# Batch 3's keys turned by transposing transfers instead of TensorE, with K and V blocks four steps apart and scores seven steps behind

## The chip, the core and the metric

The kernel runs on one core of a Trainium2 chip. A core has five engines that each work through a stream of instructions of their own, in order: TensorE (PE; its weight loads are shown as PEld), VectorE (DVE), ScalarE (ACT), GpSimd (POOL) and SyncE (SP). They meet through semaphores. Transfers run on 16 DMA engines; SyncE, ScalarE and GpSimd issue them, each in its place in that engine's stream. The metric is the time of one execution in microseconds (us), so less is better.

## The reference, cut to what matters

Selective attention over 8 batches of 8 heads, 576 positions, head size 64, and then a gated feed-forward network (FFN) on 4608 tokens of 512 values, with 1536 hidden values:

```python
scores = (1 / np.sqrt(D)) * np.matmul(q, k.transpose(0, 1, 3, 2))
cum = np.cumsum(np.maximum(s, 0.0), axis=-1)
bias = -(cum[:, :, :, None] - cum[:, :, None, :])
scores = np.where(causal, -1e9, scores + np.minimum(bias, 0.0))
attn = softmax(scores)                       # over the keys
x = np.matmul(attn, v)                       # to (4608, 512)
xn = x / np.sqrt(np.mean(x * x, axis=-1, keepdims=True) + 1e-6) * rms_g
g = xn @ w_gate
out = (g * sigmoid(g) * (xn @ w_val)) @ w_out
```

Inputs and the output are float32. The kernel multiplies in bf16.

## The kernel before, in words

**The two halves.** The FFN runs over nine chunks of 512 tokens (`ffn`). A chunk has twelve pairs of a gate group (L751) and a value group (L760) of four matmuls each, and then four output groups of twelve matmuls (L773). Between groups the code calls `step()`, 36 times a chunk, 324 times in all. The attention is cut into small pieces, and each step places a few of them. So TensorE's stream is FFN matmuls with pieces of attention between them, and the attention of a batch runs a chunk or two ahead of the FFN that reads it. A step's number is used below as a place in this order: chunk c begins after step 36 c. It is an order written by the program while it is built, not a time; the engines meet it as fast as their waits let them.

**The pieces of a batch.** A batch has five blocks of 128 positions (the last has 64). For each block of keys `kb` and half of the heads `g` there is a score piece (`s_step`, matmuls at L278, exponentials on ScalarE at L302, the causal mask on GpSimd at L311). For each block of queries `qb` and half `g` there is a value product (`av_step`, L344 and L350), whose sum is divided on VectorE (L357, L359). When both halves of a block are there, it is squared and scaled (L366, L379, L382, L389) and turned into the layout of the FFN by a transposing transfer on SyncE's queue (`xt_dma`, L400). The scores read `kqT`, in which K and Q are turned so that the head size lies along the partitions. There is one buffer for scores (`psS`), so a score waits until the exponentials of the one before have read it.

**How K and Q get into `kqT`.** There are three ways, by two constants, `XB = 2` and `KB = 4`:

- Batches 0 and 1: K and Q are loaded in float32 (`kq32`), cast to bf16 (`kqn`), turned on TensorE by four matmuls with an identity (`t_step`, L195; the tail of 64 positions in `tail_step`, L220), and copied out of PSUM by ScalarE or VectorE (L203, L227).
- Batches 2 and 3: Q is loaded in float32, cast on GpSimd (L156) and turned by transposing transfers on SyncE's queue (`kq_dma`, L182). K is loaded in float32, cast on GpSimd (L145), and turned on TensorE, four groups and a tail for a batch, each copied out by ScalarE.
- Batches 4 to 7: Q as in batches 2 and 3. K is loaded block by block by a casting transfer of GpSimd's queue (`load_k`, L162), straight into bf16, and each block is turned by a transposing transfer (`kq_dma` again).

V comes block by block from GpSimd's queue in all batches (`load_v`, L186). `kqn`, `kqT` and `v_sb` have two buffers each, by the parity of the batch.

**What sets the order.** `step()` looks at conditions on step numbers, kept in `done`. `ready(lag, key)` says that something was placed at least `lag` steps ago. Side work stands in four queues (`act_side`, `pool_side`, `dve_side`, `v_side`), of which only the head is looked at, once a step. `casts(b)` fills `pool_side` with the loads of K (`key(c)`) and the casts of Q of batch `b`; `after_av(b)` fills `v_side` with the loads of V of batch `b + 2`. `x_seq` lists the transposing transfers of K and Q, at most one in two steps, and none in a step that places an `xt_dma`. `can_s` and `can_av` hold a score or a product back until its inputs are some steps old:

```python
return all(ready(5, "X", b, 1, c) for c in (kb, min(kb + 1, 4))) and (
    ready(5, "X", b, 0, kb) if b >= KB else ready(3, "T", b) if kb >= 3 else
    all(ready(3, "T", b, hp, 0) for hp in (2 * g, 2 * g + 1)))
```

These lags only decide where an instruction stands. On the chip it still waits for the semaphore of its input, and since the streams are in order, everything behind it waits too. `need(c)` places filler matmuls where the rows for chunk `c` have not been placed in time.

Of the kernel before, what the change touches and what calls it, by code (L numbers as in the profile page):

```python
# [26 lines left out]
def kernel(  # L27
# [13 lines left out]
    B, H, S, D = q.shape  # L41
# [5 lines left out]
    NSC = 5  # L47
# [6 lines left out]
    def rows(c):  # L54
        return 128 if c < 4 else 64
# [25 lines left out]
    kqTn = kqT.rearrange("d a w (h n) -> d a w h n", h=HP)  # L81
    kqTx = kqT.rearrange("d a w (c h n) -> d a w c h n", c=NSC, h=HP)
    XB = 2
    KB = 4
    v_sb = mp.tile([128, 2, NSC, H, NV], BF16, name="v_sb")

    NE = 8
# [72 lines left out]
    def load_k(b, c):  # L160
        n = rows(c)
        nc.gpsimd.dma_start(  # L162
            out=kqn[0:n, b % 2, 0, c],
            in_=k[b, :, c * 128:c * 128 + n, :].rearrange("h p d -> p h d"))
# [19 lines left out]
    def load_v(b, c):  # L184
        n = rows(c)
        nc.gpsimd.dma_start(  # L186
            out=v_sb[0:n, b % 2, c, :, 0:64],
            in_=v[b, :, c * 128:c * 128 + n, :].rearrange("h p d -> p h d"))
# [53 lines left out]
    def slot_free():  # L242
        return eread.get(ecount[0] % NE, 0) == 0
# [5 lines left out]
    def s_step(b, kb, g, pair=None, masked=False):  # L249
# [181 lines left out]

    SLOTS = 36
    K2 = 34
    slot = [0]
    first, chunk = [0], [0]
    done = {}
    last = {"S": -9, "AV": -9, "T": -9, "X": -9, "AVT": -9, "L": -9}
    s_seq = [(b, kb, g) for b in range(B) for kb in range(NSC) for g in (0, 1) if kb < 4 or g == 0]
    s_seq.sort(key=lambda x: (1, 0, x[2], x[1]) if x[0] == 1 and x[1] < 2 else (x[0], x[1], x[2], 0))
    av_seq = [(b, qb, g) for b in range(B) for qb in range(NSC) for g in (0, 1)]  # L440
    xt_seq = [(b, qb) for b in range(B) for qb in range(NSC)]
    t_seq = [(b, hp, w) for b in range(KB) for hp in list(range(HP)) + ["tail"]
             for w in (0, 1) if w == 0 or (hp != "tail" and b < XB)]
# [22 lines left out]
    def early(queue, lag, fns):  # L466

        t = slot[0] + lag
        queue.extend((lambda: slot[0] >= t and phase() < 24, f) for f in fns)

    def check(b, ws=(1, 0)):
        t = slot[0] + (8 if b >= KB else 0)

        def when(w):
            if b < 2:
                return slot[0] % 2 and chunk[0] == b and slot[0] > 16
            return phase() >= 25 and slot[0] >= t and (w == 0 or ready(0, "cast", b, 1))
        dve_side.extend((lambda w=w: when(w), f) for w in (ws if b < KB else (0, 1)) for f in (
            lambda w=w: check_mag(b, w), lambda: check_max(0), lambda: check_max(1),
            lambda w=w: done.__setitem__(("check", b, w), slot[0])))  # L480

    def phase():

        return slot[0] - first[0]

    def loads(b, w, when, lag):

        def main():
            load_kq(nc.scalar, b, w)
            last["L"] = slot[0]  # L490

        def tail():
            load_kq_tail(nc.scalar, b, w)
            done["raw", b, w] = last["L"] = slot[0]
        n = len(act_side)
        when(act_side, lag, [main, tail])
        act_side[n:] = [(lambda c=c: c() and slot[0] - last["L"] >= 3, f) for c, f in act_side[n:]]

    def casts(b):

        def key(c):
            load_k(b, c)
            done["K", b, c] = slot[0]
            if c == NSC - 1:
                check(b)

        def over(w):
            done["cast", b, w] = slot[0]  # L510
            if b + 1 < B and (w == 1 or b + 1 < KB):
                loads(b + 1, w, early, 4)
            if w == 1:
                x_seq.extend((b, ww, c) for c in range(NSC) for ww in ((1, 0) if b >= KB else (1,)))
            else:
                done["cast", b] = slot[0]
                check(b)

        def free(w):
            return ready(0, "check", b - 2, w) and (  # L520
                ready(0, "T", b - 2) if w == 0 and b < KB + 2 else
                b < XB + 2 or ready(4, "X", b - 2, w, 4))
        if b >= KB:
            pool_side.extend((lambda: free(0) and slot[0] % 2 == 0, lambda c=c: key(c)) for c in range(NSC))
        fns = [(1, lambda r=r: cast_x(nc.gpsimd, b, 1, r)) for r in range(NSC)]
        if b == 2:
            fns[-1] = (1, lambda: (cast_x(nc.gpsimd, b, 1, NSC - 1), over(1)))
        else:
            fns += [(1, lambda: over(1))]
        if b < KB:  # L530
            fns += [(0, lambda r=r: cast(nc.gpsimd, b, 0, r, r + 1)) for r in range(NSC)]
            fns += [(0, lambda: over(0))]
        if b == 2:

            def put2(queue, *fs):
                queue.extend((lambda: slot[0] >= K2 and free(0) and free(1), f) for f in fs)
            put2(act_side, *[lambda r=r: cast_x(nc.scalar, b, 1, r) for r in (3, 4)],
                 *[lambda r=r: cast(nc.scalar, b, 0, r, r + 1) for r in (0, 1, 2)])
            put2(pool_side, *[lambda r=r: cast_x(nc.gpsimd, b, 1, r) for r in (0, 1)],
                 lambda: (cast_x(nc.gpsimd, b, 1, 2), over(1)),  # L540
                 lambda: cast(nc.gpsimd, b, 0, 3, 4), lambda: (cast(nc.gpsimd, b, 0, 4, 5), over(0)))
            return
        pool_side.extend((lambda w=w: ready(7, "raw", b, w) and free(w), f) for w, f in fns)

    def after_tail(b):
        if b + 2 < B:
            casts(b + 2)

    def after_av(b):
        if b + 2 < B:  # L550
            if b == 0:
                v_side.extend((lambda: chunk[0] == 1, f) for f in (
                    lambda: (load_v(2, 0), load_v(2, 1)), lambda: (load_v(2, 2), load_v(2, 3)),
                    lambda: (load_v(2, 4), done.__setitem__(("V", 2), slot[0]))))
                return
            early(v_side, 6, [lambda r=r: load_v(b + 2, r) for r in range(NSC)]
                  + [lambda: done.__setitem__(("V", b + 2), slot[0])])

    def do_t(key, **kw):
        b, hp, w = key  # L560
# [58 lines left out]
    def can_s():  # L619
        if not s_seq or not slot_free():  # L620
            return False
        b, kb, g = s_seq[0]
        if b == 1 and (phase() < 24 and phase() % 2 == 0 or kb == 4 and at("AV", 1, 3, 1) > slot[0]):
            return False
        due = SLOTS * ((b * S + kb * 128) // DM) - (26 if b == 1 else 18 if b < 4 else 14)
        if slot[0] - last["S"] < (4 if slot[0] < due - 24 else 3 if slot[0] < due else 2):
            return False
        if b >= XB:
            return all(ready(5, "X", b, 1, c) for c in (kb, min(kb + 1, 4))) and (
                ready(5, "X", b, 0, kb) if b >= KB else ready(3, "T", b) if kb >= 3 else  # L630
                all(ready(3, "T", b, hp, 0) for hp in (2 * g, 2 * g + 1)))
        if kb >= 3 and not ready(3, "T", b):
            return False
        if kb == 4:
            return True
        return all(ready(3, "T", b, 2 * g + j, w) for j in (0, 1) for w in (0, 1))

    def can_av(clear=False):
        if not av_seq:
            return False  # L640
        b, qb, g = av_seq[0]
        if slot[0] - last["AV"] < (1 if (b, qb) == (1, 3) else 2):
            return False
        if b > 0 and g == 1 and slot[0] - last["T"] < 3 and not clear:
            return False
        if b > 1 and not ready(8, "V", b):
            return False
        if qb > 0 and not ready(5, "S", b, qb - 1, g):
            return False
        prev = b * NSC + qb - NX  # L650
        if prev >= 0 and at("XT", prev // NSC, prev % NSC) > slot[0]:
            return False
        return ready(4 if (b, qb) == (1, 3) else 5, "S", b, qb, g)
# [582 lines left out]
```

## Time and profile before

| what | value |
|---|---|
| median of 3 runs | 365.96 us (365.79 to 369.27) |
| the profiled execution | 364.69 us, of which the span of the trace is 363.0 us |
| granted TensorE clock in it | 0.999 |
| TensorE | 2383 matmuls |
| transposing transfers of K and Q (L182) | 50 |
| transposing transfers of normalised rows (L400) | 36 issues in the page's list |
| casting loads of K blocks (L162) | 20 |
| loads of V blocks (L186) | 40 |

In a row of a group of instructions stand the line, the engine, the operation, what is written and read, the shapes, how often, the busy time and the mean of one, and the idle time of the engine just ahead with what ended it. In a row of the timeline stand the start and the length in us. Matmuls overlap, so the start of the next one says more than the length of this one. A row of a transfer gives the queue, how many, the size, and the median time from issue to landing.

### The profile page before, as it was taken

What the parts mean: (1) busy time and instruction counts of PE and PEld (TensorE: products, weight loads), DVE (VectorE), ACT (ScalarE), POOL (GpSimd) and SP (SyncE); (2) the same over time, 40 slices, a digit from 0 to 9 for tenths busy, and PEclk for the clock granted to TensorE, in tenths of its full rate; (3) what the DMA queues carried; (4) which work ended last, traced back from release to release, by engine and by line L of the source; (5) the groups of instructions that cost most, each with busy time, mean ns of one, the idle gap of its engine ahead of it and who ended that gap; (6) DMA issues with size and microseconds to landing.
All of it is one profiled execution on the core that took longest, in us unless ns stands there. A gap on an engine that the chain in (4) does not pass through costs nothing. (4 is left out here: it accounts for less than half of the span.)

```text
span 363.0 us, 6976 instructions
## 1 busy us (share of the span) xinstructions
PE 348.8 (96%) x2383; PEld 160.5 (44%) x2383; DVE 273.4 (75%) x523; ACT 239.8 (66%) x619; POOL 178.2 (49%) x283
## 2 busy tenths in 40 slices
PE   4989999999999999999999999999999999999993
PEld 2445444444445444444444444444444444444441
DVE  6697988698888889788998988884588548827820
ACT  3988884768886778877778768776777653223311
POOL 7959765858865566869737954622232200000000
PEclk9999999999999999999999999999999999999999
DMA  7999999999969399969979994973201130020011
GB/s 228 132 229 256 177 170 259 182 201 193 212 127 138 59 198 138 167 147 163 164 202 124 140 142 105 115 85 90 78 14 17 51 103 1 0 88 29 1 60 60
DMA packets 124096, 45.81 MB, mean 126 GB/s; under 512 B 103956, under 2 KB 118808, under 8 KB 124056
## 3 DMA queue, kind: packets, MB, share of 16 engines
q0 software_dynamic: 62688, 14.29, 47.4%
q1 hardware_dynamic: 51872, 23.80, 32.1%
q10 hardware_dynamic: 9496, 7.23, 8.4%
q8 instruction: 19, 0.31, 0.4%
q14 instruction: 21, 0.17, 0.2%
HBM read 37.90 MB, written 9.44 MB: 130 GB/s over the span
## 5 line engine op out<-in xcount | busy, mean ns | idle before, releaser
L302 ACT ACTIVATE E<-psS,biasK 128x256 bf16<-128x256 f32 (+3 forms) x328 | 107.0, 415 | 18.9 <-PE psS L278 18.6
L751 PE MATMUL psF<-xnT,wg_sb 128*128 128x512 bf16 x432 | 111.1, 379 | 0.6 <-ACT xnT L416 0.3
L760 PE MATMUL psF<-xnT,wv_sb 128*128 128x512 bf16 x432 | 111.1, 379 | 0.0
L773 PE MATMUL psF<-wout_sb,Ht 128*128 128x512 bf16 x432 | 102.5, 379 | 0.1
L763 DVE SCALAR_TENSOR_TENSOR U<-T,psF 128x512 bf16<-128x512 f32 x108 | 73.7, 682 | 29.4 <-ACT T L754 29.4
L754 ACT ACTIVATE T<-psF 128x512 f32<-128x512 f32 x108 | 64.4, 596 | 41.0 <-PE psF L751 38.6
L311 POOL TENSOR_SCALAR_AFFINE_SELECT E<-E 128x512 bf16<-128x512 bf16 x64 | 46.5, 727 | 77.5 <-ACT E L302 77.0
L756 DVE TENSOR_TENSOR Ht<-U,psF 128x512 bf16<-128x512 bf16 x99 | 67.7, 684 | 7.0 <-PE psF L760 0.5
L751 PEld LDWEIGHTS <-wg_sb 128*128 128x128 bf16 x432 | 38.7, 98 | 44.9 <-issue 5.6
L773 PEld LDWEIGHTS <-Ht 128*128 128x128 bf16 x432 | 38.6, 97 | 42.4 <-issue 2.3
L760 PEld LDWEIGHTS <-wv_sb 128*128 128x128 bf16 x432 | 38.5, 98 | 42.2 <-issue 4.2
L778 ACT ACTIVATE osb<-psF 128x512 f32<-128x512 f32 x36 | 21.5, 596 | 32.0 <-PE psF L773 25.5
L389 DVE SCALAR_TENSOR_TENSOR xs_sb<-x_sb,al_all,g_row 128x512 bf16<-128x512 bf16 (+1 forms) x36 | 29.9, 831 | 12.8 <-POOL al_all L382 12.1
L186 POOL DMA_DIRECT2D v_sb<-in_v_dram x40 | 35.4, 888 | 0.7 <-PE psAV L350 0.3
L366 ACT ACTIVATE xs_sb<-x_sb 128x512 bf16<-128x512 bf16 (+1 forms) x37 | 23.5, 636 | 17.9 <-DVE x_sb L359 17.5
L427 DVE TENSOR_TENSOR acc<-acc,mag 128x1280 bf16<-128x1280 bf16 x32 | 26.6, 845 | 0.2
L278 PE MATMUL psS<-kqT 64*128 64x256 bf16 (+2 forms) x304 | 25.9, 256 | 0.9 <-ACT kqT L203 0.5
L350 PEld LDWEIGHTS <-E 128*128 128x128 bf16 x320 | 21.7, 98 | 10.0 <-issue 0.2
L379 POOL TENSOR_SCALAR al_all<-ss_all 128x1 f32<-128x1 f32 (+2 forms) x39 | 10.7, 274 | 29.7 <-ACT xs_sb L366 22.9
L382 POOL TENSOR_TENSOR al_all<-al_all,mhalf 128x1 f32<-128x1 f32 (+2 forms) x39 | 22.2, 570 | 3.2
L344 PEld LDWEIGHTS <-E 128*128 128x128 bf16 x256 | 20.0, 98 | 8.6 <-DVE x_sb L359 1.6
L278 PEld LDWEIGHTS <-kqT 64*128 64x128 bf16 x320 | 9.2, 94 | 30.8 <-issue 29.9
(126 smaller groups left out, 301.0 us busy)
## 6 DMA issues: line engine op xcount, KB each, us to landing
out_dram<-osb SPq DMA_DIRECT2D x36, 256.0 KB, 2.3
kq<-in_q_dram ACTq DMA_DIRECT2D x5, 1024.0 KB, 6.2
v_sb<-in_v_dram POOLq DMA_DIRECT2D x32, 128.0 KB, 6.4
kq<-in_k_dram SPq DMA_DIRECT2D x4, 512.0 KB, 5.6
kq<-in_q_dram SPq DMA_DIRECT2D x4, 512.0 KB, 7.5
kqn<-in_k_dram POOLq DMA_DIRECT2D x16, 128.0 KB, 5.4
wout_sb<-in_moe_w_out_dram POOLq DMA_DIRECT2D x2, 768.0 KB, 9.9
kq<-in_q_dram POOLq DMA_DIRECT2D x1, 1024.0 KB, 10.8
```

The lines of the kernel that those rows point to most:

```text
L186: nc.gpsimd.dma_start(out=v_sb[0:n, b % 2, c, :, 0:64], in_=v[b, :, c * 128:c * 128 + n, :].rearrange("h p d -> p h d"))
L278: nc.tensor.matmul(pair[par][:, j * W:j * W + M], lhsT=kT, rhs=qT, start=(j == 0 and not premask), stop=(j == nj - 1))
L302: nc.scalar.activation(out=eo, in_=ei, func=AF.Exp, scale=0.125, bias=biasK[:, kb, bh:bh + 1])
L311: nc.gpsimd.affine_select(out=Ev[:, :, 0:nq], in_=Ev[:, :, 0:nq], pattern=[[0, nh], [1, nq]], compare_op=ALU.is_ge, fill=0.0, base=0, chan ...
L389: nc.vector.scalar_tensor_tensor(out=xs_sb[0:n, (b * NSC + qb) % NX, :], in0=x_sb[0:n, (b * NSC + qb) % NX, :], scalar=al_all[0:n, col:col ...
L427: nc.vector.tensor_tensor(out=acc[:, sl], in0=acc[:, sl], in1=mag[:, sl], op=ALU.max)
L751: nc.tensor.matmul(Gp, lhsT=wg_sb[:, cc, fs], rhs=xnT[:, cc, x0:x0 + DM], start=(cc == 0), stop=(cc == CC - 1))
L754: nc.scalar.activation(out=T, in_=Gp, func=AF.Tanh, scale=0.5)
L756: nc.vector.tensor_tensor(out=Ht[:, fb - 1, :], in0=pend[0], in1=pend[1], op=ALU.mult)
L760: nc.tensor.matmul(Vp, lhsT=wv_sb[:, cc, fs], rhs=xnT[:, cc, x0:x0 + DM], start=(cc == 0), stop=(cc == CC - 1))
L763: nc.vector.scalar_tensor_tensor(out=U, in0=T, scalar=1.0, in1=Gp, op0=ALU.add, op1=ALU.mult)
L773: nc.tensor.matmul(Op, lhsT=Ht[:, fb, tb * 128:(tb + 1) * 128], rhs=wout_sb[:, fb, :], start=(fb == 0), stop=(fb == FB - 1))
```

## The change

`KB` goes from 4 to 3. Batch 3's K is then handled like that of batches 4 to 7: five casting loads and five transposing transfers in place of one float load with its tail, five casts, five groups of transposes on TensorE and five copies. Batch 3's K loads stand behind its Q casts in `pool_side`; those of batches 4 to 7 stand ahead of the casts, as they did.

A new constant `SPREAD = 4` sets the least number of steps between two blocks of K, and between two blocks of V for batches 4 to 7; for batch 3 blocks of V stay two steps apart. Before, both could go every second step. A product now waits for the V block that it reads and not for the last one of the batch. Scores of batches from `KB` on stand at least seven steps behind the transfers of K and Q that they read, instead of five.

```diff
-    KB = 4
+    KB = 3
...
     K2 = 34
+    SPREAD = 4
...
-    last = {"S": -9, "AV": -9, "T": -9, "X": -9, "AVT": -9, "L": -9}
+    last = {"S": -9, "AV": -9, "T": -9, "X": -9, "AVT": -9, "L": -9, "K": -9, "V": -9}
...
         def key(c):
             load_k(b, c)
+            last["K"] = slot[0]
             done["K", b, c] = slot[0]
...
-        if b >= KB:
-            pool_side.extend((lambda: free(0) and slot[0] % 2 == 0, lambda c=c: key(c)) for c in range(NSC))
+        keys = [(lambda: free(0) and slot[0] % 2 == 0 and slot[0] - last["K"] >= SPREAD, lambda c=c: key(c))
+                for c in range(NSC)] if b >= KB else []
+        if b > KB:
+            pool_side.extend(keys)
...
         pool_side.extend((lambda w=w: ready(7, "raw", b, w) and free(w), f) for w, f in fns)
+        if b == KB:
+            pool_side.extend(keys)
...
     def after_av(b):
...
-            early(v_side, 6, [lambda r=r: load_v(b + 2, r) for r in range(NSC)]
-                  + [lambda: done.__setitem__(("V", b + 2), slot[0])])
+            t0 = slot[0] + 6
+
+            def block(r):
+                load_v(b + 2, r)
+                done["V", b + 2, r] = last["V"] = slot[0]
+            v_side.extend((lambda: slot[0] >= t0 and phase() < 24 and slot[0] - last["V"] >= (SPREAD if b > 1 else 2),
+                           lambda r=r: block(r)) for r in range(NSC))
...
         if b >= XB:
-            return all(ready(5, "X", b, 1, c) for c in (kb, min(kb + 1, 4))) and (
-                ready(5, "X", b, 0, kb) if b >= KB else ready(3, "T", b) if kb >= 3 else
+            lag = 7 if b >= KB else 5
+            return all(ready(lag, "X", b, 1, c) for c in (kb, min(kb + 1, 4))) and (
+                ready(lag, "X", b, 0, kb) if b >= KB else ready(3, "T", b) if kb >= 3 else
...
-        if b > 1 and not ready(8, "V", b):
+        if b > 1 and not ready(8, "V", b, qb):
```

More of the change, by code (lines that the diff above doesn't have):

```diff
@@ L551, in after_av, with block @@
             if b == 0:
-                v_side.extend((lambda: chunk[0] == 1, f) for f in (
-                    lambda: (load_v(2, 0), load_v(2, 1)), lambda: (load_v(2, 2), load_v(2, 3)),
-                    lambda: (load_v(2, 4), done.__setitem__(("V", 2), slot[0]))))
-                return
-            early(v_side, 6, [lambda r=r: load_v(b + 2, r) for r in range(NSC)]
-                  + [lambda: done.__setitem__(("V", b + 2), slot[0])])
+                def block(*rs):
+                    for r in rs:
+                        load_v(2, r)
+                        done["V", 2, r] = last["V"] = slot[0]
+                v_side.extend((lambda: chunk[0] == 1, lambda rs=rs: block(*rs)) for rs in ((0, 1), (2, 3), (4,)))
+                return
+            t0 = slot[0] + 6
[4 more added lines that the diff above has]
+                           lambda r=r: block(r)) for r in range(NSC))
     def do_t(key, **kw):
```

## The prediction

> **What bounds the kernel now.** The page comes first: span, busy time by engine, and the slices.
>
> ```profile
> span 363.0 us, 6976 instructions
> ...
> PE 348.8 (96%) x2383; PEld 160.5 (44%) x2383; DVE 273.4 (75%) x523; ACT 239.8 (66%) x619; POOL 178.2 (49%) x283
> ...
> PE   4989999999999999999999999999999999999993
> ...
> DMA  7999999999969399969979994973201130020011
> ```
>
> TensorE is busy 96% of the span, and the lost tenths lie in the first slices. The DMA engines are nearly as full up to slice 21, so a transfer that is added there competes with others. Since a busy TensorE need not be a fully used one, I read its stretches next; the columns are the stretch, its length, then busy time and instructions of PE, PEld, DVE, ACT and POOL, clock, DMA share and GB/s.
>
> ```profile
> 69.00:107.00 38.00, 37.84 (x267) 17.54 (x265) 33.23 (x59) 30.27 (x81) 26.61 (x38) 1.00 1.37 180
> 107.00:146.00 39.00, 38.68 (x283) 17.86 (x281) 33.26 (x61) 28.67 (x78) 24.58 (x38) 1.00 1.19 136
> 146.00:184.00 38.00, 38.00 (x272) 17.04 (x271) 31.99 (x59) 28.65 (x82) 29.14 (x45) 1.00 1.40 162
> ```
>
> From 146 us on TensorE has no idle time at all, at full clock, and no other engine is above 33 of 38 us. So TensorE's instruction stream, which is in order, is the bound: an instruction taken out of it is gained one for one, and a wait put into it is lost one for one. What is left to win by waits is the 0.16 us and 0.32 us idle of the two earlier stretches, plus waits too short to count as idle, which show only from start to start in the timeline.
>
> **The change part by part.** I take the steps from the order of the instructions in the two built programs. The changed one has exactly 20 matmuls fewer and no other more (no filler from `need`).
>
> *Transposes removed.* Batch 3's four K transposes (L195, four matmuls each) and its tail (L220, four) are all of their kind in this stretch:
>
> ```profile
> L195 PE MATMUL psT<-ident_bf,kqn 128*128 128x128 bf16 x16 | 1.5, 219 | 0.0
> ...
> L220 PE MATMUL psT<-ident_bf,kqn 128*128 128x128 bf16 x4 | 0.4, 219 | 0.0
> ```
>
> ```profile
> 101.72 0.39 PE L195 MATMUL psT<-ident_bf,kqn 128*128 128x128 bf16 x4
> 101.94 1.03 PE L773 MATMUL psF<-wout_sb,Ht 128*128 128x512 bf16 x4
> ```
>
> A group of four stands 0.39 us in the record, but the next matmul starts 0.22 us after it, because the ends overlap. Five groups by 0.22 us give 1.1 us; the busy column (1.5 + 0.4 = 1.9 us) is the upper bound. I take 1.1, since starts are what an in-order engine pays.
>
> [...]
>
> *Short waits of batch 3's scores.* In the old order these scores stand two steps apart (steps 89, 91, 93, 95), because the ones ahead of them (steps 73 and 86) stood far apart, waiting for the transposes at steps 77 to 85.
>
> ```profile
> 121.19 0.39 PE L278 MATMUL psS<-kqT 64*128 64x256 bf16 x4
> 121.67 1.02 PE L751 MATMUL psF<-xnT,wg_sb 128*128 128x512 bf16 x4
> ...
> 125.55 1.03 PE L751 MATMUL psF<-xnT,wg_sb 128*128 128x512 bf16 x4
> 126.64 0.40 PE L278 MATMUL psS<-kqT 64*128 64x256 bf16 x4
> 126.97 1.04 PE L760 MATMUL psF<-xnT,wv_sb 128*128 128x512 bf16 x4
> 127.84 0.29 PE L350 MATMUL psT<-v_sb,E 128*128 128x65 bf16 x4
> 127.97 1.02 PE L751 MATMUL psF<-xnT,wg_sb 128*128 128x512 bf16 x4
> 128.93 0.39 PE L278 MATMUL psS<-kqT 64*128 64x256 bf16 x4
> ...
> 130.37 1.03 PE L751 MATMUL psF<-xnT,wg_sb 128*128 128x512 bf16 x4
> 131.56 0.39 PE L278 MATMUL psS<-kqT 64*128 64x256 bf16 x4 [0.17 <-ACT E L302]
> ```
>
> Undisturbed, four FFN matmuls ahead of a score take 0.96 us (127.97 to 128.93) and the score 0.33 us (126.64 to 126.97). Beyond that stand 0.15 us at 121.19 (0.48), 0.13 at 125.55 (1.09) and 0.23 at 130.37 (1.19): 0.5 us together. The named releaser is ScalarE's exponentials, which still read the one score buffer. The new order puts these scores at steps 75, 78, 82, 85, 89, 91, 96, 100 and 103, with one two-step pair left, and ScalarE has five evictions less to do. So I take the whole 0.5 us as gone; none gone is the other bound.
>
> *Side engines.* ScalarE loses five evictions of transposes; at 66% busy that counts only where a score waits for it, and is in the 0.5 us above. On GpSimd come and go:
>
> ```profile
> L162 POOL DMA_DIRECT2D kqn<-in_k_dram x8 | 7.5, 941 | 0.0
> ...
> L145 POOL CAST kqn<-kq 128x512 bf16<-128x512 f32 x4 | 3.0, 751 | 0.0
> ```
>
> GpSimd loses five casts of about 0.75 us and gains five load issues of 0.94 us, 1 us more in all, at 49% busy. A load issue that waits (for the check or the score that last read its buffer) holds back the masks queued behind it, and so the value products; those stand five steps behind their score, which covers a wait of some 5 us. I cost this at nothing.
>
> *Added transfers, and the first new wait.* Batch 3's K no longer comes as one float load through ScalarE's queue (step 46) but as five casting loads through GpSimd's (steps 56, 60, 64, 68, 72), and five transposing transfers join SyncE's queue (steps 64, 70, 80, 87, 94). Past these stand the transfers of the normalised rows that the next FFN chunk reads. The tightest is the one issued at step 67, which chunk 2 needs:
>
> ```profile
> 103.90 1.19 SPq L400 DMA_TRANSPOSE xnT<-xs_sb  x1
> 105.18 1.23 SPq L182 DMA_TRANSPOSE kqT<-kqn  x1
> ```
>
> ```profile
> xnT<-xs_sb SPq DMA_TRANSPOSE x1, 2.4
> ```
>
> ```profile
> xnT<-xs_sb SPq DMA_TRANSPOSE x2, 6.8
> ```
>
> ```profile
> 107.06 1.03 PE L751 MATMUL psF<-xnT,wg_sb 128*128 128x512 bf16 x4
> 108.01 0.39 PE L278 MATMUL psS<-kqT 64*128 64x256 bf16 x4
> ```
>
> It was issued at 103.90 and landed 2.4 us later, at 106.3; chunk 2 reads it at 107.06, a margin of 0.76 us. Two removed groups (steps 67 and 70) bring the reader 0.44 us nearer: 0.32 us are left. The loads of K now run beside it. In the crowded stretch from 69 to 94 us such transfers took 6.8 us, so the wait lies between 0 and 4.1 us; I take 0.5, near the quiet row, because there is one K block per four steps.
>
> *The second new wait.* The first scores of four blocks of batch 3, and of two blocks of batch 4, now stand exactly seven steps after the last transfer that they need (scores at steps 75, 82, 89, 96, 112, 121). Score (3,0,0) stood at step 73 (108.01) and (3,0,1) at step 86 (121.19): 13.2 us for 13 steps, so seven steps are 7.1 us. Of these SyncE takes a part:
>
> ```profile
> 102.81 0.19 PE L344 MATMUL psAV<-v_sb,E 128*128 128x65 bf16 x1
> ```
>
> Step 68 stands on TensorE at 102.81, and the transfer of that step was issued at 105.18, 2.4 us later, behind an output and a row transfer. What remains is 4.7 us; where SyncE is free it is 7.1. The times to land, of 94 to 147 us, of 121 to 134 us, where V blocks come two steps apart, and of all:
>
> ```profile
> kqT<-kqn SPq DMA_TRANSPOSE x12, 4.7
> ```
>
> ```profile
> kqT<-kqn SPq DMA_TRANSPOSE x3, 7.2
> ```
>
> ```profile
> DMA to landing us min/median/max: 2.3/4.7/11.4
> ```
>
> So the median just fits the shorter allowance, and the crowded value just fits the longer. Bounds for a score are 0 (2.3 lands inside both) and 11.4 - 4.7 = 6.7 us. I take 0.1 us a score, 0.6 us in all, since the medians lie at the edge and not beyond it.
>
> *The spreading.* Blocks of K and V of batches 4 to 7 are issued four steps apart instead of two; their transposes come 7 to 14 steps later than before and their scores 2 to 7. The cover is distance: from batch 5 on a score stands 11 steps or more behind its last transfer, 11 us for 2.4 in the queue and 4.7 to land. The latest V block (batch 6, step 185) has 29 steps before its product. The last product moves from step 249 to 251 of 324, and the rows that each later chunk needs are out eight steps ahead or more. I cost it at nothing; if that cover were gone, each late score would cost what a score of batch 3 can.
>
> Sum: -1.1 - 0.5 + 0.5 + 0.6 = **-0.5 us**. The profiled execution took 364.69 us (363.0 of span and 1.7 around it), so 364.2; its time stands 1.3 us under the median of the timed runs, 365.96, so against those I forecast 365.5 us.
>
> **The rivals.**
>
> *No new wait.* Transfers land inside their allowance, because loads spread out lower the crowding. For it: the float load that filled the stretch before 92 us is gone, and one K block per four steps is little. Against: the margin of 0.32 us. It gives -1.6 us: 364.4 us.
>
> *The transposes are late, slower.* Place: the six scores at seven steps, TensorE waiting at L278 for kqT. Price: if K and V blocks together (steps 83 to 95) make 7.2 us the usual landing, and half of the scores have the short allowance, three wait 7.2 - 4.7 = 2.5 us; with 2.0 us at the start of chunk 2 this is 9.5 - 1.6 = +7.9 us, 373.9 us. It decides from 1.6 us of waits together, 0.27 us a score; past 1% it takes 5.3 us. For it: the row of 7.2 us. Against: from 69 us on the old TensorE waits nowhere long on a transfer. [...]
>
> *Gain above 1%.* All idle time after 69 us (0.16 + 0.32), the 0.5 us of short waits and 1.9 us of transposes make 2.9 us, under 3.7. Only noise gets there.
>
> **How the numbers follow.** A change under 1% (3.7 us) can't be told from none by a measurement of this kernel. Forecast, small gain partly given back (364.5 to 366.5): 0.45. No new wait (363.5 to 364.5): 0.25. Late transposes inside 1% (366.5 to 369.6): 0.16. Late beyond it: 0.11. Above 1% faster: 0.03. So faster 0.03, same 0.86, slower 0.11. The range 363.5 to 369.3 leaves out 0.03 below and 0.12 above.
>
> **What would show it.** Right: 20 matmuls fewer, TensorE busy near 347 us, the starts around L278 of batch 3 at 0.96 and 0.33 us, and at most one or two idle entries "PE psS <- DMA kqT" under 1 us. The start of chunk 2 has its own row: PE or PEld at the gate matmul, released by DMA xnT. Wrong: idle time of several us at L278 released by DMA kqT, landing times of kqT above 7 us between 105 and 160 us, or a wait at value products released by DMA v_sb, which I cost at nothing.

## The result and the profile after

The changed kernel takes 370.74 us (median of four runs, 369.64 to 371.59), the kernel before beside it 366.05 us: a ratio of 1.013 [1.009, 1.017]. The forecast was 365.5 us with a range of 363.5 to 369.3, so the time lies above the range, on the side of the rival "late transposes". Measured a second time, the ratio was 1.017 [1.012, 1.021].

The profiled execution of after took 371.59 us, 370.0 of them span, at a mean granted clock of 0.986. That is 7.0 us of span more than in the profile of before; the medians lie 4.7 us apart, since the profiled execution of before lies under its median and that of after above its own. First the page of after: span, busy time by engine, the slices of TensorE and of its clock, and the group of score matmuls.

```profile
span 370.0 us, 6936 instructions
...
PE 350.7 (95%) x2363; PEld 160.3 (43%) x2363; DVE 275.4 (74%) x523; ACT 237.9 (64%) x614; POOL 178.1 (48%) x283
...
PE   5989999989999999599999999999999999999993
...
PEclk9999999999999999799999999999999999999998
...
L278 PE MATMUL psS<-kqT 64*128 64x256 bf16 (+2 forms) x304 | 26.1, 258 | 6.2 <-DMA kqT<-kqn 5.5
```

The group of score matmuls in before:

```profile
L278 PE MATMUL psS<-kqT 64*128 64x256 bf16 (+2 forms) x304 | 25.9, 256 | 0.9 <-ACT kqT L203 0.5
```

The 20 matmuls are gone (2383 to 2363), but TensorE's busy time has gone up by 1.9 us instead of down. Both tell where to look: slice 17 (148 to 157 us) has half of TensorE idle and the clock at 0.7. TensorE now stands idle 6.2 us ahead of scores instead of 0.9, and 5.5 of these end with a transfer into `kqT`. The waits of TensorE between 69 and 190 us, as engine, line, releaser, then total, times and longest:

```profile
PE psS L278 <- DMA kqT<-kqn: 5.5, 2, 4.4
PE psF L765 <- DVE U L777: 0.7, 1, 0.7
PE psF L765 <- DMA xnT<-xs_sb: 0.3, 1, 0.3
PE psS L278 <- ACT E L302: 0.2, 1, 0.2
```

In before the same stretch has one entry:

```profile
PE psS L278 <- ACT E L302: 0.3, 2, 0.2
```

The stretches of after, with the columns of the prediction's, show that most of the loss is in one place:

```profile
107.00:148.00 41.00, 40.72 (x288) 18.47 (x287) 34.71 (x65) 28.89 (x78) 27.72 (x41) 1.00 0.94 116
...
153.40:158.90 5.50, 5.49 (x16) 1.78 (x16) 1.38 (x2) 2.16 (x5) 1.38 (x2) 0.53 1.75 162
```

In the 41 us of the first row TensorE lost 0.28 us. Then comes the wait, and after it 5.5 us in which TensorE is busy without a gap, at a clock of 0.53. The timeline of TensorE in after:

```profile
78.69 0.39 PE L278 MATMUL psS<-kqT 64*128 64x256 bf16 x4 [1.11 <-DMA kqT<-kqn]
...
107.82 1.02 PE L765 MATMUL psF<-xnT,wg_sb 128*128 128x512 bf16 x4 [0.28 <-DMA xnT<-xs_sb]
...
153.41 0.61 PE L278 MATMUL psS<-kqT 64*128 64x256 bf16 x4 [4.44 <-DMA kqT<-kqn]
153.95 1.89 PE L765 MATMUL psF<-xnT,wg_sb 128*128 128x512 bf16 x4
155.63 1.91 PE L774 MATMUL psF<-xnT,wv_sb 128*128 128x512 bf16 x4
157.34 1.63 PE L765 MATMUL psF<-xnT,wg_sb 128*128 128x512 bf16 x4
158.90 0.39 PE L278 MATMUL psS<-kqT 64*128 64x256 bf16 x4
...
171.00 1.02 PE L765 MATMUL psF<-xnT,wg_sb 128*128 128x512 bf16 x4 [0.75 <-DVE U L777]
```

The instruction that waits 4.44 us is score (4,0,0), the first of batch 4, at step 112. Behind it a group of four FFN matmuls takes 1.7 us from start to start (153.95, 155.63, 157.34). At full clock it is 0.87 us, or 0.96 us with a score behind it. From 153.41 to 158.90 the work of 0.33 + 0.87 + 0.87 + 0.96 = 3.0 us took 5.5 us, so the low clock cost 2.5 us more. A wait of 4.4 us therefore cost 6.9 us in this execution. All four runs of the second measurement had the same mean clock of 0.986; the other three of the first had 0.994, so there the stretch of low clock was shorter or absent, and the 2.5 us hold for the profiled execution.

Why score (4,0,0) waits can be read backwards. It needs the transposing transfer of step 105. TensorE passed step 105 here:

```profile
142.04 0.19 PE L344 MATMUL psT<-v_sb,E 128*128 128x65 bf16 x1
```

SyncE's queue in after, whose columns are start and length of an issue:

```profile
142.07 1.22 SPq L182 DMA_TRANSPOSE kqT<-kqn  x1
...
144.01 1.21 SPq L182 DMA_TRANSPOSE kqT<-kqn  x1
...
145.90 1.23 SPq L182 DMA_TRANSPOSE kqT<-kqn  x1
```

The last one is the transfer of step 105, issued 3.9 us after TensorE had passed that step, behind other transposing transfers of 1.2 us each and two output transfers. The transfers that were issued between 145.5 and 149 us, with size and time from issue to landing:

```profile
kq<-in_q_dram ACTq DMA_DIRECT2D x1, 1024.0 KB, 7.3
...
kqn<-in_k_dram POOLq DMA_DIRECT2D x2, 128.0 KB, 11.5
...
v_sb<-in_v_dram POOLq DMA_DIRECT2D x1, 64.0 KB, 11.7
kqT<-kqn SPq DMA_TRANSPOSE x1, 7.5
```

It landed 7.5 us later, at 153.4. TensorE was ready for the score at 153.41 - 4.44 = 148.97, which is 6.9 us after step 105, so the seven steps did give about seven microseconds. The sum 3.9 + 7.5 - 6.9 = 4.5 is the wait.

What is new at that place is the large load. Batch 5's Q is one transfer of 1 MB (and a tail of 128 KB three steps later), issued by ScalarE here in after:

```profile
146.26 0.40 ACTq L129 DMA_DIRECT2D kq<-in_q_dram  x1
```

and in before 22 us earlier:

```profile
124.54 0.43 ACTq L129 DMA_DIRECT2D kq<-in_q_dram  x1
```

In step numbers it moved from 89 to 109. The order of the two built programs shows how. Batch 4's K blocks stand ahead of batch 4's Q casts in `pool_side`, where only the head is looked at. With four steps between them these blocks go out at steps 76 to 92, and the casts behind them move from steps 80 to 84 back to 93 to 97. The load of batch 5's Q needs the buffer that the casts free, and it may only go out in the first 24 steps of a chunk. By step 97 chunk 2 (steps 73 to 108) is past that, so the load waits for the start of chunk 3 and stands at step 109. There it runs beside the transfer that the tightest score of batch 4 needs.

The account of the span, from start to start in the two timelines (so the two gate groups and score (2,0,0) stand with a little more than the idle time of their rows; the row of the 20 transposes is the prediction's figure):

| place in after | us |
|---|---|
| wait of score (4,0,0) | +4.4 |
| half clock after it | +2.5 |
| score (2,0,0) at 78.69, the same order in both programs up to there | +1.2 |
| start of chunk 2 (107.82) | +0.45 |
| gate group at 171.00, behind an instruction of VectorE that took 2.8 us | +0.9 |
| 20 transposes | -1.1 |
| short waits of batch 3's scores | -0.5 |
| before step 37, where the programs are alike | -0.6 |
| sum, against 7.0 of span | +7.3 |

### The profile page after: what moved, and what is told of

It is laid out like the page before. It is cut to its first block, busy times and chain, and to the rows that moved or that the text cites. A ratio compares the mean times of both kernels' runs of the same rounds, so it can differ in the third digit from the quotient of the medians.

```text
span 370.0 us, 6936 instructions
## 1 busy us (share of the span) xinstructions
PE 350.7 (95%) x2363; PEld 160.3 (43%) x2363; DVE 275.4 (74%) x523; ACT 237.9 (64%) x614; POOL 178.1 (48%) x283
## 5 line engine op out<-in xcount | busy, mean ns | idle before, releaser
L765 PE MATMUL psF<-xnT,wg_sb 128*128 128x512 bf16 x432 | 112.4, 383 | 1.3 <-DVE U L777 0.7
L311 POOL TENSOR_SCALAR_AFFINE_SELECT E<-E 128x512 bf16<-128x512 bf16 x64 | 44.0, 688 | 92.9 <-ACT E L302 85.0
L278 PE MATMUL psS<-kqT 64*128 64x256 bf16 (+2 forms) x304 | 26.1, 258 | 6.2 <-DMA kqT<-kqn 5.5
L382 POOL TENSOR_TENSOR al_all<-al_all,mhalf 128x1 f32<-128x1 f32 (+2 forms) x39 | 24.1, 617 | 3.3
L278 PEld LDWEIGHTS <-kqT 64*128 64x128 bf16 x320 | 9.2, 94 | 36.3 <-issue 33.6
L162 POOL DMA_DIRECT2D kqn<-in_k_dram x25 | 23.4, 937 | 0.2 <-issue 0.2
```

The costliest lines, as they stand in the source:

```text
L278: nc.tensor.matmul(pair[par][:, j * W:j * W + M], lhsT=kT, rhs=qT, start=(j == 0 and not premask), stop=(j == nj - 1))
L311: nc.gpsimd.affine_select(out=Ev[:, :, 0:nq], in_=Ev[:, :, 0:nq], pattern=[[0, nh], [1, nq]], compare_op=ALU.is_ge, fill=0.0, base=0, chan ...
L765: nc.tensor.matmul(Gp, lhsT=wg_sb[:, cc, fs], rhs=xnT[:, cc, x0:x0 + DM], start=(cc == 0), stop=(cc == CC - 1))
```

## The experiments

The theory was that the moved 1 MB load makes the transfer of step 105 late, and that the half clock follows from the length of the wait. The first rival was that seven steps are too few for a transposing transfer here in any case. The second was that the transposing transfers of batch 3 themselves cost it.

**More distance.** Scores stand eleven steps behind their transfers instead of seven.

```diff
-            lag = 7 if b >= KB else 5
+            lag = 11 if b >= KB else 5
```

> The whole change, with the scores of batches 3 to 7 at least eleven steps behind their transfers instead of seven; nothing else differs. Theory (late transposes): the changed kernel loses 4.4 us where score (4,0,0) waits for kqT at the start of chunk 3, and about 2 us by the half clock that follows; with four steps more the transfers have landed, no wait at L278 for DMA kqT is over 1 us in batches 3 to 7, no stretch of half clock follows, and the time is 364 to 366 us. Rival (the added traffic as such slows the whole middle of the kernel, the long wait is only where it surfaces): waits appear elsewhere, and the time stays above 368 us.

368.22 us, ratio 1.007 [1.004, 1.009]. The long wait goes, as the theory had it, but 2.4 us of loss against before stay: the time lies above the theory's 364 to 366 us and just inside the rival's range. The profiled execution (372.63 us) was the slowest of the ten, with waits of 1.1 and 2.3 us before 39 us already, so there is a second profile:

> A second look at the whole change with the lag of eleven (368.2 us, 3 us over the version that also puts Q's casts first): the first profile was of an execution disturbed before step 37. Theory (what is left is the burst at the start of chunk 3): waits of some 2 us in all between 140 and 175 us, at VectorE's and ScalarE's results or at a value product. Rival: waits spread over the whole middle.

That execution took 366.83 us. No wait on `kqT` is left; a new one stands at the end of batch 3 (1.01 us in the first profile too), with some of 0.3 us each at VectorE's results behind it, as the theory expected. On the timelines of TensorE, ScalarE and VectorE of this kernel:

```profile
142.11 0.29 PE L278 MATMUL psS<-kqT 64*128 64x64 bf16 x8 [1.00 <-ACT E L302]
```

```profile
139.00 0.63 ACT L366 ACTIVATE xs_sb<-x_sb 128x512 bf16<-128x512 bf16 x1 [1.93 <-DVE x_sb L359]
```

```profile
135.41 3.00 DVE L427 TENSOR_TENSOR acc<-acc,mag 128x1280 bf16<-128x1280 bf16 x2
```

The last scores of batch 3 stand at steps 99, 102 and 105 here, exactly as in before, so it is not that they are closer together. There is one score buffer, and the score waits for ScalarE's exponentials. These stand behind a squaring that waits 1.93 us for VectorE, where two instructions took 3.00 us. In the fastest version below the same two took 1.55 us. Beside them in this kernel, between 135.40 and 137.73, GpSimd works through a row of two casts and a mask; the casts are those of batch 4's Q, at the later steps that the spacing gives them. So distance cures the late transfer, while the moved casts seem still to cost; the last section has more of this. No edit tests it by itself.

**Each part alone.** First the spacing and the lag without batch 3's transfers (`KB = 4`), then the transfers and the lag without the spacing.

```diff
-    KB = 3
+    KB = 4
```

> KB back at 4: batch 3's keys turned on TensorE as before, while the spreading to four steps and the lag of seven stay. Theory (late transposes): the twenty TensorE transposes come back (+1.1 us against the changed kernel) and score (4,0,0) stands at step 108 as before, eight steps behind its transfer and ahead of the loads that chunk 3 releases; no long wait there, 365 to 367.5 us. Rival (spreading is what makes the transfers late): the wait of several us stays, at (4,0,0) or at (5,0,0), which is now also seven steps behind, and the time is 368 to 371 us.

```diff
-    SPREAD = 4
+    SPREAD = 2
```

> SPREAD 2 instead of 4: batch 3's keys by transposing transfers and the lag of seven stay, but blocks of K and V go out two steps apart as before. Theory (a tight score meets a burst of loads): score (4,0,0) stands at step 110, seven behind its transfer at 103, still with the loads released at the start of chunk 3 close by: a wait of 1 to 4 us, 366 to 370 us. Rival (spreading pushed blocks of V and K over the end of chunk 2, and these are the burst): without spreading the burst is gone, no wait over 1 us, 364 to 365.5 us.

The spacing alone took 376.31 us, ratio 1.030 [1.022, 1.037], above what either theory or rival gave it and 5.6 us above the whole change. Neither had foreseen where it loses. The waits of TensorE in it, from 69 to 326 us:

```profile
PE psF L765 <- DVE U L777: 4.0, 4, 2.3
PE psS L278 <- DMA kqT<-kqn: 3.9, 3, 1.6
```

Without batch 3's blocks the queue comes out otherwise: it is batch 6's Q load that misses its window, and goes out at step 145, the start of chunk 4. Three scores wait for transfers and four gate groups for VectorE, the longest of them 2.3 us. The last section has what ran beside VectorE's late instruction at the longest of them.

The transfers without the spacing took 371.68 us, ratio 1.014 [1.008, 1.020], as much as the whole change, and above what theory and rival gave it. Its waits in the same stretch:

```profile
PE psS L278 <- DMA kqT<-kqn: 3.1, 2, 2.3
PE psF L765 <- DMA xnT<-xs_sb: 2.0, 1, 2.0
```

Here the start of chunk 2 waits 2.0 us for normalised rows; with the spacing it was 0.28 us in the first profile, and none to 0.75 us in four others of the same order up to there. So the spacing does seem to protect that place, and loses its gain at another. The wait of 2.3 us for `kqT` stands at 138.26, at a score of batch 3: the Q load is at its old step 89 here, beside the transposing transfer of batch 3 of that step, which took 7.2 us to land.

**Only the one load moved.** Batch 5's Q load, with its tail, is held until step 114, behind the transfer in question. The order is otherwise the same up to step 114; behind that, the casts of this Q and the next Q load follow it.

```diff
-        act_side[n:] = [(lambda c=c: c() and slot[0] - last["L"] >= 3, f) for c, f in act_side[n:]]
+        act_side[n:] = [(lambda c=c: c() and slot[0] - last["L"] >= 3 and (b != 5 or slot[0] >= 114), f)
+                        for c, f in act_side[n:]]
```

> The whole change, but the float load of batch 5's Q (1 MB, released at step 109, the start of chunk 3) is held until step 114, two steps behind score (4,0,0). Theory (the burst beside the transfer makes it late): the transfer issued at step 105 lands in about 4 to 5 us instead of 7.5, the wait at score (4,0,0) falls from 4.4 us to under 2, the half clock does not come, and the time is 365 to 367.5 us. Rival (the transfer is late because SyncE issues it 4 us after its step, behind rows that wait for VectorE's checks): the wait stays over 3 us and the time at 369 to 371 us.

367.32 us, ratio 1.003 [0.999, 1.006]. This is the run that decides between the theory and the first rival: the loads of K and V beside the transfer are the same as in after, and only the Q load with its tail is gone. The transfer of step 105 in it, and then the timeline of TensorE at score (4,0,0) and at the next long wait:

```profile
kqT<-kqn SPq DMA_TRANSPOSE x1, 4.3
```

```profile
150.99 0.39 PE L278 MATMUL psS<-kqT 64*128 64x256 bf16 x4 [1.31 <-DMA kqT<-kqn]
...
195.33 0.39 PE L278 MATMUL psS<-kqT 64*128 64x256 bf16 x4 [2.83 <-DMA kqT<-kqn]
```

Without the load beside it the same transfer lands in 4.3 us instead of 7.5, and the wait shrinks by as much, from 4.4 to 1.3 us. The 7.5 us is no chance of one execution: in the second profile of after, which has the load there too, it is 7.5 us again (issued at 146.10, its score at 153.59). What remains is SyncE's lateness. The rest of the gain is not had: with Q 5 late, batch 6's Q load moves to step 145, and a score waits 2.83 us at 195.33. After that wait the clock stays at 1.00.

**The wait filled.** Twenty filler matmuls are added ahead of score (4,0,0), more work that computes nothing. They can't make the transfer earlier; they only keep TensorE busy while it waits.

```diff
+        if key == (4, 0, 0):
+            warm(20)
```

> The whole change, with twenty filler matmuls (216 ns each, 4.3 us) on TensorE just ahead of score (4,0,0), in the place of the wait; nothing else differs. Theory (the wait of 4.4 us at this score lets the clock fall): the fillers lie inside the wait, the eleven matmuls behind it run at 216 ns and not at 427, and the time is 1 to 2.5 us under the changed kernel: 368 to 369.7 us. Rival (the half clock has another cause, or costs nothing since transfers bound the next steps anyway): no gain, 370 to 372 us.

369.57 us, ratio 1.008 [1.005, 1.011]. Repeated beside the changed kernel itself, on one chip:

> The changed kernel once more, beside the same runs of the kernel before as the next three. Theory: the wait of 3 to 5 us at score (4,0,0) with a stretch of half clock behind it comes again, 369.5 to 371.5 us; the transfer of step 105 lands 7 us or more after its issue. Rival (that execution was a chance): the long wait stands elsewhere or not at all in this profile.

> The twenty fillers ahead of score (4,0,0) once more, beside the changed kernel. Theory: 1 to 2.5 us under the changed kernel of the same call (the half clock's 2.1 us, less what the fillers overrun the wait). Rival: within 0.5 us of it.

The changed kernel took 371.43 us (370.92 to 373.54) and the one with fillers 369.91 (368.57 to 370.58): 1.5 us less with more work. The changed kernel again shows its wait, on its timeline of TensorE:

```profile
153.59 0.61 PE L278 MATMUL psS<-kqT 64*128 64x256 bf16 x4 [4.45 <-DMA kqT<-kqn]
```

and the kernel with fillers shows the same stretch filled:

```profile
150.16 4.48 PE L690 MATMUL psF<-mneg,ident_bf 128*128 128x512 bf16 x20
154.85 0.40 PE L278 MATMUL psS<-kqT 64*128 64x256 bf16 x4 [0.21 <-DMA kqT<-kqn]
155.18 1.04 PE L767 MATMUL psF<-xnT,wg_sb 128*128 128x512 bf16 x4
156.05 1.03 PE L776 MATMUL psF<-xnT,wv_sb 128*128 128x512 bf16 x4
```

The score still starts 4.7 us after the stream before it has ended (150.16 to 154.85), but the group behind it takes 0.87 us, full clock. So the half clock was a cost of its own, and it went when the idle time was filled. By length, the waits read in these traces sort as follows. Waits of 2.34 us (the version without the spacing) and 2.83 us (the one load moved) left the clock at full, with 0.87 us for the four matmuls of the group behind them. Behind 3.57 us (the queue turned round, below), 4.44 us (the profile of after) and 5.46 us (batch 3's transfers alone, below) such a group took 1.68 to 1.69 us. One wait does not fit so simply: early in the first profile with a lag of eleven, 2.31 us brought the half clock as well, as its timeline of TensorE and a stretch of it (clock 0.50, in the column behind the engines) show:

```profile
38.67 0.38 PE L195 MATMUL psT<-ident_bf,kqn 128*128 128x128 bf16 x4 [2.31 <-ACT kqT L203]
```

```profile
39.40:42.70 3.30, 3.30 (x19) 1.62 (x18) 2.21 (x5) 2.49 (x6) 1.26 (x3) 0.50 1.68 130
```

So the length of the wait alone does not decide, and what else does is left open here. The longest wait did not have the longest stretch either: behind 5.46 us TensorE worked at half clock for 2.8 us, behind 4.44 us for 5.1 us.

**Batch 3's transfers alone, on the kernel before.** No spacing, no lag of seven.

```diff
-    KB = 4
+    KB = 3
```

> The kernel before with KB = 3 alone: no spreading, lag of five, products wait for the whole V of a batch. Theory (a transposing transfer needs 6 to 9 us from its step to its landing where loads run beside it): the first scores of batch 3's blocks stand five steps, 5 us, behind their transfers, each waits 1 to 3 us, and the time is 370 to 376 us. Rival (what costs is the spreading and not the way by transfers): 364 to 367 us.

380.59 us, ratio 1.038 [1.030, 1.047], the slowest of all and 4.6 us above the upper end of what was expected. Its waits, from 69 to 326 us:

```profile
PE psS L278 <- DMA kqT<-kqn: 8.7, 4, 5.5
```

With five steps of distance four scores are late, one of them by 5.5 us, and the clock falls behind it. This version lacks the lag of seven, the spacing, the new order of batch 3's K blocks and the wait for single V blocks, all at once. The version without the spacing has the other three and is 9 us faster; which of them makes that difference was not tested.

**The order in the queue turned round.** The K blocks stand behind the Q casts in all batches, as the change has it for batch 3 only. Then the casts, and with them the Q loads, keep their places.

```diff
-        if b > KB:
-            pool_side.extend(keys)
...
-        if b == KB:
-            pool_side.extend(keys)
+        pool_side.extend(keys)
```

> The whole change, but the blocks of K stand behind the casts of Q in GpSimd's side queue in all batches and not in batch 3 alone. The load of batch 5's Q then goes out at step 89 as in the kernel before, instead of step 109, the start of chunk 3; score (4,0,0) still stands seven steps behind its transfer (103 to 110). Theory (the burst of loads at the start of chunk 3 makes this transfer late): it lands within 5 us, the wait of 4.4 us falls under 1.5, and the time is 365 to 368 us. Rival (seven steps are too few there whatever runs beside): a wait of 2 us or more stays at a score of batch 4, 368 to 371 us.

369.62 us, ratio 1.008 [1.005, 1.012]: a miss, the theory had 365 to 368. The wait at (4,0,0) is gone as expected. But at step 89, to which the load returns, there stands a transposing transfer of batch 3, and it now meets the same neighbour. The timeline of ScalarE, and of TensorE, in this kernel:

```profile
124.82 0.45 ACTq L129 DMA_DIRECT2D kq<-in_q_dram  x1
```

```profile
135.73 0.61 PE L278 MATMUL psS<-kqT 64*128 64x256 bf16 x4 [3.57 <-DMA kqT<-kqn]
136.27 1.89 PE L784 MATMUL psF<-wout_sb,Ht 128*128 128x512 bf16 x4
```

That transfer, issued at 127.21, took 8.4 us to land; in after, where the load is not beside it, the same transfer was issued at 126.62 and took 4.5 us. The wait has moved with the load, and so has the half clock (1.89 us for four matmuls). Blocks of K move with this edit too, so it is the less clean of the two tests. But it points the same way as the run with the one load moved and the one without the spacing: at both places where the 1 MB load stood beside a transposing transfer with a tight score behind it, that score waited. A second score waits 1.0 us at 166.29 here.

**Both together.** The queue turned round and a lag of eleven steps.

> As the run with Q's casts first, with scores at least eleven steps behind their transfers. Theory: neither the burst nor a short lag is left, no wait for DMA kqT over 0.5 us in batches 3 to 7; what remains of the change is the gain of the twenty transposes (1.1 us) less the chunk starts that wait for normalised rows: 364 to 366 us. Rival (the added transfers cost elsewhere): 367 us or more.

365.13 us (363.76 to 366.18 in ten executions), ratio 0.997 [0.994, 1.000]. This is the fastest version, 5.6 us under the first median of the change, though its interval just reaches no difference from before. Its waits from 69 to 326 us have no entry for `kqT` at all:

```profile
PE psF L762 <- DMA xnT<-xs_sb: 2.3, 2, 1.8
PE psF L762 <- DVE U L774: 0.4, 2, 0.2
PE psS L278 <- ACT E L302: 0.2, 1, 0.2
```

The start of chunk 2 is in the first row with 0.5 us; the larger part of that row, 1.8 us, stands at 69.96, at the start of chunk 1, before the change begins to act.

**The two ways of turning batch 3's K.** The last version with batch 3's keys on TensorE again (`KB = 4`). With that constant batch 3's K comes as one float load again and its scores go back to a lag of five.

> The best version so far (Q's casts first, scores eleven steps behind: 365.1 us) with KB back at 4, so that batch 3's keys are turned on TensorE. It prices the twenty transposes by themselves, in an order without tight scores from batch 4 on. Theory: 1.1 us for the transposes and up to 0.5 for the scores of batch 3 that then stand close together: 366 to 367 us. Rival (the transfers of batch 3's keys take as much elsewhere as they save): 364.5 to 365.5 us.

366.98 us, ratio 1.002 [0.999, 1.006], against 0.997 [0.994, 1.000]. The difference of the ratios is 0.5%, some 1.9 us in favour of the transfers, though the intervals overlap and the two versions ran on different chips, each beside the kernel before. The prediction's two gains, 1.1 and 0.5 us, are of that size.

## Why the prediction was wrong, point by point

**The bound** was right. TensorE's stream is the bound, and each wait put into it was lost at least one for one. The longest was lost by more, which the prediction did not think of.

**Transposes removed (1.1 us) and short waits (0.5 us)** were right as far as the runs tell. There are 20 matmuls fewer. On after's timeline each score of batch 3 with four matmuls has 0.96 us for the four FFN matmuls ahead of it and 0.33 us for itself, so the 0.5 us are gone. The pair of runs that differs in batch 3's way gives about 1.9 us, by intervals that overlap. That TensorE's busy time would fall to 347 us was wrong, mainly since the work at half clock took 2.5 us longer.

**The first new wait**, at the start of chunk 2, was right in place and cause: 0.5 us foreseen, 0.45 lost (0.28 us idle; 0.64 us in the second profile). Its size was a choice between 0 and 4.1 us, so the close number is partly luck. The version without spacing shows 2.0 us there, inside these bounds.

**The second new wait** is the step that failed: 0.6 us in the sum, 4.4 us in the trace. The mechanism, six scores at seven steps, was named, and so was step 112. But 0.1 us a score was taken from a median of 4.7 us to land and a lateness of SyncE of 2.4 us. Five of the six scores indeed had no long wait. The sixth had 4.4 us: its transfer was issued 3.9 us late and took 7.5 us. The time to land is within what the prediction quoted (7.2 us for a crowded place, 11.4 the longest), and the wait is within its bound of 6.7 us a score; for SyncE's lateness it had one figure, 2.4 us, and no range. A median over many places was used for one place whose neighbours could have been looked up in the order of the new program.

**The spreading, "I cost it at nothing"**, is the term that failed with it, and the reason for 3.1 of the 4.4 us; the other 1.3 us is SyncE's lateness. The working looked at the K and V blocks, their own transposes and their scores, and found distance enough. It did not follow what stands behind the K blocks in `pool_side`: the casts of Q, the buffer that these free, and the window of 24 steps that the next Q load then misses. So the 1 MB load that moved by 20 steps was not in the sum at all. Holding that load back took 3.1 us off the wait. But leaving out the spreading does not save the change: without it the load stays at step 89, beside another transfer with a tight score, and that score waits 2.3 us. What was missing in both cases is the look at what runs beside each tight transfer.

**The half clock** was in no term. It added 2.5 us to a wait of 4.4 in the profiled execution, where a wait of 2.8 us in another run added none. A price per microsecond of waiting is thus too low for long waits.

**The rivals.** "The transposes are late" had place and sign, and 7.2 us to land where 7.5 were measured. It had the wrong composition: three waits of 2.5 us and 2.0 us at the start of chunk 2, against one wait of 4.4, its half clock, and 0.45. Its 373.9 us lies 3 us above the measured median. It had a chance of 0.11 beyond 1%, and that is what came. What spoke against it, that the old TensorE waits nowhere long on a transfer, said nothing about transfers and loads at new places. In this version of the change the transposing transfers lost (370.74 against 366.05 us). In the one in which the landing is covered they did not: it was 0.5% faster than its twin with transposes on TensorE, by intervals that overlap. "No new wait" (364.4 us) is about what the version with the landing covered takes, 365.13 us.

The signs listed as showing the prediction wrong did come: several microseconds idle at L278 released by `kqT`, and a landing time above 7 us between 105 and 160 us.

**Not in the prediction either**: the 0.9 us at 171.00. They seem to come from the same shift of the queue, by another way: the Q casts of batch 5, which stand between 150 and 156 us in before, now stand between 163 and 170 us, beside an instruction of VectorE that took 2.80 us there (last section). This is read from traces, and was not tested by an edit.

The wait of score (2,0,0) came in one execution of the change (1.11 us) and in that of the spacing alone (0.83 us), neither in that of before nor in the second profile of the change. The order up to there is the same in all of them, so it is not put down to the edit.

## What to carry to other kernels

When steps of an in-order side queue are moved apart, list everything queued behind them, down to the loads that wait for the buffers these free, and see in which window each then lands; here the harm was done by a load that the change does not mention. For a transfer with little distance to its reader, look up what is issued beside it at that place in the new order, and don't take the median over the kernel. A wait of TensorE of several microseconds (here from 3.57 us on, once from 2.31) has to be priced with the half clock after it; filling it with matmuls that compute nothing won that part back here, 1.5 us.

## What the runs showed of the hardware

- A small transposing transfer took 7.5 us with a 1 MB load beside it (after) and 4.3 us with that one load moved; at another place such a transfer took 8.4 us with the load beside it (the queue turned round), against 4.5 us without (after). The casting loads of 64 and 128 KB issued beside the large load in after took 11.4 to 11.7 us, and the first of them 4.5 us with that load moved.
- Waits of TensorE of 2.34 and 2.83 us left the clock at full; behind 3.57, 4.44 and 5.46 us TensorE worked at half clock for 3.3, 5.1 and 2.8 us. One wait of 2.31 us brought 3.4 us of half clock too.
- An instruction of VectorE took 2.80 us beside a row of GpSimd's without a gap. It is the scaling of the normalised rows, which takes 0.75 us in the median. On VectorE's timeline of after:

```profile
167.55 2.80 DVE L389 SCALAR_TENSOR_TENSOR xs_sb<-x_sb,al_all,g_row 128x512 bf16<-128x512 bf16 x1
```

and on GpSimd's, in the same kernel, there stand beside it

```profile
167.49 0.62 POOL L156 CAST kqn<-kq 128x512 bf16<-128x512 f32 x1
168.05 0.65 POOL L311 TENSOR_SCALAR_AFFINE_SELECT E<-E 128x512 bf16<-128x512 bf16 x1
168.64 0.61 POOL L156 CAST kqn<-kq 128x512 bf16<-128x512 f32 x1
169.19 0.61 POOL L145 CAST kqn<-kq 128x512 bf16<-128x512 f32 x1
```

GpSimd's row began 0.06 us earlier and ended at 169.80; VectorE's instruction ended 0.55 us after that, at 170.35. In the second profile and in both with fillers, where GpSimd's row is the same, it again took 2.79 to 2.80 us, and in the version with the spacing alone 3.60 us beside five such instructions, in the one without the spacing 2.22 us beside three (there the end is again 0.55 us behind GpSimd's, 159.76 and 159.21). In the versions with a lag of eleven the casts stand elsewhere and no scaling takes over 1.5 us; the two instructions of 3.00 us told of above are others, beside a like row. So beside three, four and five instructions of GpSimd the scaling took 2.22, 2.80 and 3.60 us; why is not shown, since no run moves the row alone. Its end does not always lie behind the row's: in the run with the one load moved, a scaling of 1.77 us ended 0.55 us behind the second of three casts, and there the third cast took 1.08 us instead of 0.61.
